# An S4 block and SwiGLU FFN on one core: eight blocks of two token tiles in place of two of two and four of three

## The chip, the cores and the metric

One core of one Trainium2 chip. The metric is the device time in microseconds, as the median of several runs. Engines: TensorE (PE, with PEld for its weight loads), VectorE (DVE), ScalarE (ACT), GpSimd (POOL), and SyncE (SP), which here only issues DMAs.

## What is computed

2048 tokens of 448 channels pass through a state-space convolution and then a gated feed-forward network (FFN), each behind a layer norm that is modulated by a condition c.

```python
sa, ca, ga, sb, cb, gb = (silu(c) @ w_mod) in six parts
h = layernorm(x) * (1 + ca) + sa
x = x + ga * (causal_conv(h, K(A, B, C, dt)) + h * Dskip)
h = layernorm(x) * (1 + cb) + sb
x = x + gb * ((silu(h @ w_gate) * (h @ w_up)) @ w_down)      # 448 -> 1792 -> 448
```

## The kernel before, in words

The tokens are 16 tiles of 128. `BLOCKS` (L26) groups them into blocks, `TILES` (L27) lists each block's tiles, and `MB` (L28) sizes the buffers for the largest block. The FFN goes through its 1792 hidden units in NF = 14 groups of 128, called f.

**The FFN of one block** is `ffn` (L736). For each f, `gate_up` (L741) makes gate and up: 22 products on TensorE (L758) with weights as the stationary operand and the block's transposed tokens as the moving one, 256 columns wide for two tiles and 384 for three. Tokens and weights are split into a high and a low part, so there are 7 products with `hhi` and 4 with `hlo` for each of the two sides. They land in two PSUM buffers taken in turn from four (`bank`, L71). After them ACT takes silu (L773), DVE multiplies gate by up (L788), ACT rounds to `phi` (L795) and DVE makes the rest `plo` (L796). `down` (L800, L808) then multiplies the hidden units of the group before, f - 1, by the down weights: three products of 448 columns for each tile, summed over all f in one PSUM buffer `dn` for each tile. At the block's end DVE multiplies by the gate row and adds to x (L869, L870) and SP stores the tile (L871). A two-tile operand lies from column 32 of `hhi` and `hlo` on, a three-tile one from column 0 (`first_col`, L147).

**The last block** has another end. The down products of the last two groups are kept out of the running sum; `last_sums` (L820) adds the rest to x early, and `finish` (L826, products L836, sums L847) makes the remaining ones, the last tile in two column ranges A and B so that its store starts earlier.

**The next block's preparation** is threaded between these groups. `run_blocks` (from L885) fills a table `todo`: under (f, 0) stands what is issued between `gate_up(f)` and `down(f - 1)`, under (f, 1) what follows `down(f - 1)`. In the tuple `TIMES` a slot h means f = h // 2 and late part h % 2. An entry for a block has the slots of the first norm's statistics, of its root, and one list for each tile of the next block: the stages s0 to s5 of the convolution's recurrence (`small_path`, L941 to L1011) and then the second norm's statistics. Stage s4 has three TensorE products for each tile (L982 to L984). Stage s5 sends the running state to the next tile by a DMA (L1005). Block 0 uses the first entry, block 1 the second, later ones the third (L896).

**Transposed tokens** come in two ways. If an entry has two more elements (`late`), the second norm is finished for all tiles together, `make_xn` (L207) writes normalized rows, and `transposes` (L222) turns them on TensorE by 128x128 transposes (L227) after the last `gate_up`. Without them, each tile goes by itself: statistics and root at slot h, `make_xn` at h + 1, and `turn` (L233) at h + 2: DVE transposes 32x32 squares (L236), SP writes the tile to DRAM (L237) and reads it back in four pieces (L239). Then `split_turned` (L242) stands at f = 13 in place of `transposes`. Both end in `parts` (L218): ACT writes `hhi` (L219) and DVE writes `hlo` (L220), for each of four groups of channels.

**Order of the queues.** Each engine executes its instructions in the order written, and SP its DMAs: the loads of x for the next block at (0, 1), then the turns, then the stores at the block's end. A start-up part, before 31.7 us in the trace, makes the convolution's constants and the first block's tokens.

Of the kernel before, what the change touches and what calls it, by code (L numbers as in the profile page):

```python
# [16 lines left out]
L, D, N, F = 2048, 448, 256, 1792  # L17
# [4 lines left out]
NF = F // 128  # L22
NP0 = 3
WU = (14, 0)
NS = 3
BLOCKS = [2, 2, 3, 3, 3, 3]  # L26
TILES = [list(range(sum(BLOCKS[:b]), sum(BLOCKS[:b + 1]))) for b in range(len(BLOCKS))]  # L27
MB = max(BLOCKS)  # L28

TIMES = (
# [3 lines left out]
)  # L36

EXTRA = (1,)
# [18 lines left out]
def tile_kernel(ctx, tc, x, a_re, a_im, b_re, b_im, c_re, c_im, log_dt,  # L57
# [9 lines left out]

    DN = [psd.tile([128, 512], F32, name=f"dn{q}") for q in range(MB)]
    CV = psd.tile([128, 512], F32, name="cv")

    def bank():  # L71
        t = psg.tile([128, 512], F32, name="bank")
        return t
# [20 lines left out]

    xbuf += stage_d[0:2 * MB - 4]
    spare = stages_.rearrange("p q a b c -> p (q a b c)")
    t_of = [spare[:, q * 512:(q + 1) * 512] for q in range(2, 2 + MB + 1)]
    turned = spare[:, 1024:1024 + MB * 512].rearrange("p (q a k r) -> p q a k r", q=MB, a=4, k=4)
    xn_of = [t_of[q] for q in (2, 3, 1)]
    p_of = [spare[:, q * 512:q * 512 + MB * 128] for q in range(2)]  # L100

# [45 lines left out]
    first_col = lambda n: 32 if n == 256 else 0  # L147
    hhi = const.tile([128, 4, MB * 128], F32R)
    hlo = const.tile([128, 4, MB * 128], F32R)
# [584 lines left out]
    def run_blocks(pools, stages, first=None):  # L734
        work, hid = pools.work, pools.hid
        def ffn(ts, fresh, last, todo):  # L736
# [73 lines left out]
            m = len(ts) - 1  # L810
# [13 lines left out]
                    ve.tensor_tensor(xs[i], dn[q][:, 0:D], xs[i], op=OP.add)  # L824

            def finish():  # L826
                o = [bank(), bank(), CV, DN[0]]
                A, B = slice(0, 256), slice(256, D)
                part = [(0, slice(0, D)), (1, slice(0, D)), (m, A), (m, B)]

                def sums(f, ks):
                    (hi, lo), (wh, wl) = pp[f], wp[f]
                    for k in ks:
                        q, c = part[k]
                        for z, (u, v) in enumerate(((hi, wh), (hi, wl), (lo, wh))):
                            pe.matmul(o[k][:, c], u[:, q * 128:(q + 1) * 128], v[:, c],  # L836
                                      start=f == NF - 2 and z == 0, stop=f == NF - 1 and z == 2)

                sums(NF - 2, (0, 1))
                sums(NF - 1, (0,))  # L840
                sums(NF - 2, (2,))
                sums(NF - 1, (1, 2))
                sums(NF - 2, (3,))
                sums(NF - 1, (3,))
                for k, (q, c) in enumerate(part):
                    i = ts[q]
                    ve.tensor_tensor(xs[i][:, c], o[k][:, c], xs[i][:, c], op=OP.add)  # L847
                    if k == 2:
                        sc.dma_start(out[i * 128:(i + 1) * 128, c], xs[i][:, c])

            for f in range(NF):
# [13 lines left out]
            if last:  # L865
                return finish()
# [250 lines left out]
```

## Time and profile before

| | |
|---|---|
| median of 3 runs | 471.46 us (470.68 to 472.36) |
| profiled execution: time | 470.78 us |
| profiled execution: span | 469.0 us |
| mean granted TensorE clock | 0.997 |
| instructions | 7027 |
| DMA over the span | 31.24 MB, mean 67 GB/s |

The span runs from the first to the last instruction of the profiled execution. Three views are used: the profile's page (busy time of each engine and groups of equal instructions with count, busy us, mean ns, and the idle time before them), the chain of waits (each piece with start, length and line, in order of time), and the timeline of one engine. "out<-in" names the tiles; `raw` is also the name under which the buffers of hidden units and of turned tokens appear, since they lie in that tile. Starts on TensorE in the chain are up to 0.2 us later than in the timeline, because the chain counts from the modelled end of the piece before.

### The profile page before, as it was taken

The page shows a single profiled execution, that of the slowest core. Times are in us where ns is not written, and L with a number is a line of the kernel's source. Part 1 is how long each engine was busy: PE and PEld are TensorE (multiplying, and loading weights), DVE is VectorE, ACT ScalarE, POOL GpSimd, SP SyncE. Part 2 cuts the span into 40 slices and gives each one's busy share as a digit, 9 for nine tenths or more (in the row PEclk, how much of TensorE's full clock was granted, in tenths as well). Part 3 has the DMA queues.
Part 4 walks back from the last instruction along what each step waited for, and adds up shares of the span by engine and source line. Part 5 has one row for each costly group of instructions (what it writes and reads, how often), then busy time and mean ns, then how long its engine had stood idle before and what let it go on. Part 6 is the DMA issues. An engine that isn't in the chain of part 4 may idle for free.

```text
span 469.0 us, 7027 instructions
## 1 busy us (share of the span) xinstructions
PE 459.0 (98%) x2735; PEld 438.0 (93%) x2735; DVE 282.1 (60%) x539; ACT 160.5 (34%) x363; POOL 63.4 (14%) x88
## 2 busy tenths in 40 slices
PE   6899999999999999999999999999999999999995
PEld 4579999999999999999999999999999999999995
DVE  4888999778866447573754766374566543222225
ACT  5888666522343122233212223311223222221111
POOL 1232001000000223200022410003141000000000
PEclk9999999999999999999999999999999999999998
DMA  8976652110003000111300011130001112000001
GB/s 309 405 251 189 211 178 91 58 42 2 2 0 100 0 1 0 46 46 46 117 2 0 2 45 46 45 119 1 1 16 31 46 45 80 22 1 1 1 0 64
DMA packets 18778, 31.24 MB, mean 67 GB/s; under 512 B 2608, under 2 KB 13488, under 8 KB 18736
## 3 DMA queue, kind: packets, MB, share of 16 engines
q1 hardware_dynamic: 18096, 30.53, 19.3%
q8 instruction: 23, 0.38, 0.4%
q10 hardware_dynamic: 640, 0.18, 0.2%
q14 instruction: 19, 0.16, 0.1%
HBM read 24.61 MB, written 6.03 MB: 65 GB/s over the span
## 4 chain that ended last, share of the span: by engine, by line
PE 95%; issue 2%; DMA 1%; POOL 0%; ACT 0%; DVE 0%; POOLq 0%; ACTq 0%
PE bank L758 61%; PE dn L808 28%; DMA vec<-in_c_log_dt_dram 1%; PE dn L480 1%; PE bank L983 1%; PE cv L982 1%; PE bank L836 1%; PE cv L984 1%; PE bank L227 0%; PE bank L266 0%; PE bank L403 0%; PE cv L995 0%; PE bank L437 0%; ACT L339 0%; PE cv L375 0%
## 5 line engine op out<-in xcount | busy, mean ns | idle before, releaser
L758 PE MATMUL bank<-hhi,gu 128*128 128x384 f32 (+1 forms) x1176 | 208.9, 317 | 0.1
L758 PEld LDWEIGHTS bank<-hhi,gu 128*128 128x128 f32 x1176 | 189.4, 188 | 3.0 <-issue 0.8
L758 PE MATMUL bank<-hlo,gu 128*128 128x384 f32 (+1 forms) x672 | 130.8, 317 | 0.0
L758 PEld LDWEIGHTS bank<-hlo,gu 128*128 128x128 f32 x672 | 109.1, 188 | 0.2
L788 DVE TENSOR_TENSOR bank<-raw,bank 128x384 f32<-128x384 f32 (+1 forms) x69 | 36.9, 534 | 117.9 <-PE bank L758 115.4
L795 ACT CAST phi<-bank 128x384 fp32r<-128x384 f32 (+1 forms) x83 | 36.7, 443 | 137.9 <-DVE bank L788 137.9
L773 ACT ACTIVATE raw<-bank 128x384 f32<-128x384 f32 (+1 forms) x70 | 32.8, 469 | 119.4 <-PE bank L758 103.7
L796 DVE TENSOR_TENSOR plo<-bank,phi 128x384 fp32r<-128x384 f32 (+1 forms) x83 | 42.5, 512 | 37.5 <-ACT phi L795 37.5
L808 PE MATMUL dn<-wdh,phi 128*128 128x448 f32 x218 | 57.6, 365 | 0.0
L808 PE MATMUL dn<-wdh,plo 128*128 128x448 f32 x218 | 57.2, 363 | 0.0
L808 PE MATMUL dn<-wdl,phi 128*128 128x448 f32 x218 | 56.9, 362 | 0.0
L808 PEld LDWEIGHTS dn<-wdh,plo 128*128 128x128 f32 x218 | 40.8, 187 | 3.0 <-DVE plo L796 0.3
L808 PEld LDWEIGHTS dn<-wdl,phi 128*128 128x128 f32 x218 | 40.9, 187 | 2.7
L808 PEld LDWEIGHTS dn<-wdh,phi 128*128 128x128 f32 x218 | 38.7, 188 | 1.6 <-ACT p L773 0.2
L185 POOL TENSOR_SCALAR rsb<-mvb 128x1 f32<-128x1 f32 (+2 forms) x13 | 4.4, 337 | 142.6 <-DVE mvb L157 142.6
L125 DVE TENSOR_TENSOR gu<-raw,gu 128x1024 fp32r<-128x1024 f32 x14 | 17.0, 1218 | 0.9 <-ACT gu L123 0.9
L185 POOL TENSOR_SCALAR rsa<-mva 128x3 f32<-128x3 f32 (+1 forms) x6 | 2.3, 380 | 98.4 <-DVE mva L157 96.1
L957 POOL TENSOR_TENSOR m<-m,gm 128x448 f32<-128x448 f32 x9 | 10.4, 1155 | 20.8 <-DVE m L202 17.1
L971 DVE TENSOR_TENSOR vl<-m,vh 128x448 fp32r<-128x448 f32 x12 | 9.1, 757 | 6.7 <-ACT vh L970 6.1
L122 ACT CAST gu<-raw 128x768 fp32r<-128x768 f32 x14 | 11.6, 832 | 0.0
L976 POOL TENSOR_TENSOR m<-m,gd 128x448 f32<-128x448 f32 x9 | 11.5, 1281 | 0.0
L215 ACT ACTIVATE raw<-raw,rsb 128x64 f32<-128x64 f32 x14 | 4.8, 345 | 18.9 <-DVE raw L212 9.7
(237 smaller groups left out, 411.7 us busy)
## 6 DMA issues: line engine op xcount, KB each, us to landing
raw<-in_B_w_gate_up_dram SPq DMA_DIRECT2D x14, 512.0 KB, 3.8
rawd<-in_B_w_down_dram SPq DMA_DIRECT2D x16, 224.0 KB, 3.9
x<-in_A_u_dram SPq DMA_DIRECT2D x12, 224.0 KB, 2.8
out_dram<-x SPq DMA_DIRECT2D x11, 224.0 KB, 1.9
xd<-raw SPq DMA_DIRECT2D x9, 256.0 KB, 2.0
raw<-xd SPq DMA_DIRECT2D x36, 64.0 KB, 1.9
wm<-in_w_mod_groups_dram SPq DMA_DIRECT2D x5, 448.0 KB, 8.2
wm<-in_w_mod_groups_dram SPq DMA_DIRECT2D x5, 336.0 KB, 8.2
```

The lines of the kernel that those rows point to most:

```text
L122: sc.copy(wgu[j][:, :, 0:3, :], w[:, :, 0:3, :])
L125: ve.tensor_tensor(wgu[j][:, :, 3:7, :], w[:, :, ::-1, :], f32(wgu[j][:, :, 0:4, :][:, :, ::-1, :]), op=OP.subtract)
L185: po.tensor_scalar(rs[:, 0:n], self.mv[:, 0:n, 1], EPS, None, op0=OP.add)
L758: pe.matmul(ps[s][:, 0:n], w[:, s, a], (hlo if lo else hhi)[:, k, first_col(n):first_col(n) + n], start=first and q == 0, stop=end and q = ...
L773: sc.activation(p[:, 0:n], ps[0][:, 0:n], AF.Silu)
L788: ve.tensor_tensor(ps[1][:, 0:n], p[:, 0:n], ps[1][:, 0:n], op=OP.mult)
L795: sc.copy(hi[:, 0:n], ps[1][:, 0:n])
L796: ve.tensor_tensor(lo[:, 0:n], ps[1][:, 0:n], f32(hi[:, 0:n]), op=OP.subtract)
L808: pe.matmul(dn[q][:, 0:D], u[:, cs], v, start=f == 0 and z == 0, stop=f == (NF - 3 if last else NF - 1) and z == 2)
L957: (ve if on_v else po).tensor_tensor(v, h, g, op=OP.mult)
L971: ve.tensor_tensor(vl, v0, f32(vh), op=OP.subtract)
L976: (ve if on_v else po).tensor_tensor(h, h, gd, op=OP.mult)
```

## The change

All blocks have two tiles, so there are eight blocks instead of six. `MB` stays 3, and so do all buffers. The first entry of `TIMES`, for block 0, is the same. The second, for block 1, loses its last two elements and its third tile, so block 2 is now prepared by `turn` and `split_turned` like the later ones; the third entry has the same slots as the second. `finish` is written for any number m + 1 of tiles: m whole tiles in banks, then the two column ranges of the last tile in CV and DN[0]. With two tiles its product order is: tile 0 of group 12, tile 0 of group 13, range A of groups 12 and 13, range B of groups 12 and 13.

```diff
-BLOCKS = [2, 2, 3, 3, 3, 3]
+BLOCKS = [2] * 8
 TILES = [list(range(sum(BLOCKS[:b]), sum(BLOCKS[:b + 1]))) for b in range(len(BLOCKS))]
-MB = max(BLOCKS)
+MB = 3
...
 TIMES = (
     ((1, 3), 5, ((5, 10, 13, 15, 15, 16), (9, 9, 17, 19, 20, 20)), 20, (22, 23)),
-    ((2, 3, 3), 3, ((5, 6, 8, 10, 10, 11, 13), (7, 8, 14, 15, 17, 17, 18), (13, 17, 17, 18, 20, 21, 21)), 23, (23, 23, 23)),
-    ((2, 3, 3), 3, ((5, 6, 8, 9, 10, 11, 12), (7, 8, 13, 14, 15, 16, 17), (11, 12, 18, 18, 20, 21, 21))),
+    ((2, 3), 3, ((4, 5, 7, 8, 10, 11, 12), (7, 8, 13, 14, 16, 17, 18))),
+    ((2, 3), 3, ((4, 5, 7, 8, 10, 11, 12), (7, 8, 13, 14, 16, 17, 18))),
 )
...
             def finish():
-                o = [bank(), bank(), CV, DN[0]]
+                o = [bank() for _ in range(m)] + [CV, DN[0]]
                 A, B = slice(0, 256), slice(256, D)
-                part = [(0, slice(0, D)), (1, slice(0, D)), (m, A), (m, B)]
+                part = [(q, slice(0, D)) for q in range(m)] + [(m, A), (m, B)]
...
-                sums(NF - 2, (0, 1))
+                sums(NF - 2, range(m))
                 sums(NF - 1, (0,))
-                sums(NF - 2, (2,))
-                sums(NF - 1, (1, 2))
-                sums(NF - 2, (3,))
-                sums(NF - 1, (3,))
+                sums(NF - 2, (m,))
+                sums(NF - 1, range(1, m + 1))
+                sums(NF - 2, (m + 1,))
+                sums(NF - 1, (m + 1,))
                 for k, (q, c) in enumerate(part):
                     i = ts[q]
                     ve.tensor_tensor(xs[i][:, c], o[k][:, c], xs[i][:, c], op=OP.add)
-                    if k == 2:
+                    if k == m:
                         sc.dma_start(out[i * 128:(i + 1) * 128, c], xs[i][:, c])
```

## The prediction

> **What bounds the kernel now.** I read the page's first table, then the chain that ended last, then the timeline of VectorE (DVE) and ScalarE (ACT) around a block's end.
>
> ```profile
> span 469.0 us, 7027 instructions
> PE 459.0 (98%) x2735; PEld 438.0 (93%) x2735; DVE 282.1 (60%) x539; ACT 160.5 (34%) x363; POOL 63.4 (14%) x88
> PE 95%; issue 2%; DMA 1%; POOL 0%; ACT 0%; DVE 0%; POOLq 0%; ACTq 0%
> ```
>
> TensorE (PE) is busy for 98% of the span and carries 95% of the chain. So two questions decide: how long TensorE's own instruction list becomes, and whether somewhere in the shorter blocks another engine comes late enough to stop it. The chain in order of time answers the first (start us, length us, what, products); x22 is one pass of gate and up over one group f of 128 hidden units, L808 the products of `down`, L227 the transposes.
>
> ```profile
> 88.49 5.18 PE bank L758 x44
> ...
> 94.88 2.52 PE bank L758 x22
> ...
> 106.02 2.52 PE bank L758 x22
> 109.14 1.20 PE dn L808 x6
> ...
> 140.07 0.33 PE bank L227 x3
> ...
> 141.60 2.41 PE dn L808 x12
> 144.01 7.63 PE bank L758 x44
> 151.64 1.80 PE dn L808 x9
> ...
> 385.47 7.63 PE bank L758 x44
> ```
>
> Block 1 (two tiles) runs from 88.49 to 144.01, 55.52 us. Blocks 2 to 4 (three tiles) run from 144.01 to 385.47, 241.46 us or 80.49 us each. The last block's products start at 385.47.
>
> **The change part by part.** All differences below are of TensorE's time unless said otherwise.
>
> *Passes of gate and up.* A three-tile pass takes 7.63 / 2 = 3.815 us. From 94.88 to 106.02 lie three full steps of f (one pass and one `down` each), 11.14 / 3 = 3.713 us; less the `down` of 1.20 a two-tile pass is 2.513 us. The four three-tile blocks hold 4 x 14 = 56 passes, 213.6 us; the six two-tile blocks that replace them hold 84, 211.1 us. So more, shorter passes are slightly cheaper here: three passes of 2.513 are 7.54, two of 3.815 are 7.63. Term: **-2.5 us**. Each pass adds its silu, product, cast and difference on ACT and DVE, hidden beside TensorE as long as they are in time (below).
>
> Beside the row of 2.513 the Trainium skill, "TensorE: Matmul & The Clock Gate", section "Back-to-back issue gap", speaks against this term: an isolated product of N columns costs about N/2.4 + 2.5 ns warm, a fixed part for each product. By that (an estimate from that page) 22 products cost 2.40 us at 256 columns and 3.57 us at 384, the exchange +1.6 in place of -2.5, and the whole change about +1.0. The rows disagree with its sign: 114.2 ns for 256 columns and 173.4 for 384.
>
> *Products of `down`.* 1.80 us for nine and 1.20 for six are both 0.20 each; their number doesn't change. Nothing.
>
> *State products* (s4, three for each tile). Between 108.54, the end of the pass at 106.02, and 109.14 they take 0.60 us. Twelve tiles before and after. Nothing.
>
> *Transposes.* Block 2 was prepared in block 1 by 12 transposes on TensorE, from 140.07 to 141.60: **-1.53 us**. In their place block 1 now does what the later blocks do. Its costs elsewhere:
>
> ```profile
> L236 DVE STREAM_TRANSPOSE raw<-raw 128x512 f32<-128x512 f32 x9 | 6.4, 706 | 3.5 <-ACT raw L216 3.5
> xd<-raw SPq DMA_DIRECT2D x9, 256.0 KB, 2.0
> raw<-xd SPq DMA_DIRECT2D x36, 64.0 KB, 1.9
> 143.85:224.33 80.48, 80.48 (x444) 78.73 (x443) 45.10 (x82) 21.53 (x44) 14.74 (x17) 1.00 0.11 35
> ```
>
> The number of turned tiles goes from 9 to 12: three more of 0.71 us on DVE, and 3 writes and 12 reads more on SP's queue. In that queue the turn stands behind the block's two loads of x and ahead of its two stores; nothing else waits there. The second tile is turned at f = 10 and used at f = 13: three steps, 11.1 us, for 2.0 + 1.9 us of landing and four issues. Hidden; with that cover gone a whole landing of 1.9 us would show at each block's end. DVE's 45.10 us for three tiles and 80.48 us are 56% (third number of the row); two tiles in about 53 us keep about that share. Hidden on average; the order within a step is the question.
>
> *The block's end.* This happens six times with the turned path in place of three. After the last pass ACT and DVE must write hhi and hlo of the next block while TensorE has only two `down`s as cover: 12 x 0.20 = 2.4 us, against 3.6 before. At 256 columns the end of block 0 shows what they need:
>
> ```profile
> 85.87 0.42 DVE L788 TENSOR_TENSOR bank<-p,bank 128x256 f32<-128x256 f32 x1
> ...
> 86.32 0.37 ACT L795 CAST phi<-bank 128x256 fp32r<-128x256 f32 x1 [0.75 <-DVE bank L788]
> 86.59 0.48 ACT L219 ACTIVATE hhi<-bank,sbc 128x256 fp32r<-128x256 f32 x1
> 87.31 0.85 ACT L219 ACTIVATE hhi<-bank,sbc 128x256 fp32r<-128x256 f32 x2
> ...
> 87.90 0.87 DVE L220 SCALAR_TENSOR_TENSOR hlo<-bank,sbc,hhi 128x256 fp32r<-128x256 f32 x2
> ```
>
> Counted from L788's start (85.87), the last hhi is there at 2.29 and the last hlo at 2.90. L788 starts about 0.26 after TensorE has gone on to the next products (460.64 against 460.38 in the finish, below), so the new pass begins at 2.40 - 0.26 = 2.14. Its k = 3 part of hhi comes six products of 0.114 later, at 2.83, and the last hlo ten products later, at 3.28. Margins 0.54 and 0.38 us: no stop. Term 0; bounds 0 and, if the sources in SBUF or a semaphore cost the margin and as much again, 0.4 each, 2.4 in all.
>
> *A slower pace at a block's start.* The two passes at 88.49 took 5.18 us, not 2 x 2.513 = 5.03. No wait stands beside them, so I don't know what sets this pace. Six more two-tile blocks start with such a pair: between 0 and 6 x 0.15 = 0.9. I take **+0.5**, the middle: the pair shown is the nearest row, but it follows transposes, which the others don't.
>
> *The queues at f = 6 and 7.* make_xn of the first tile and s2 of the second stand in one step there. Three-tile block 2 shows the chain:
>
> ```profile
> 182.69 0.18 DVE L157 BATCH_NORM_AGGREGATE mvb<-stb 128x2 f32<-128x6 f32 x1
> ...
> 183.76 0.80 POOL L186 TENSOR_TENSOR rsb<-rsb,halves 128x1 f32<-128x1 f32 x1
> 184.59 0.35 ACT L215 ACTIVATE raw<-raw,rsb 128x64 f32<-128x64 f32 x1 [3.06 <-POOL rsb L186]
> 185.55 0.55 ACT L970 CAST vh<-m 128x448 fp32r<-128x448 f32 x1
> 186.13 1.16 DVE L971 TENSOR_TENSOR vl<-m,vh 128x448 fp32r<-128x448 f32 x1 [1.48 <-ACT vh L970]
> 187.22 0.55 DVE L788 TENSOR_TENSOR bank<-raw,bank 128x384 f32<-128x384 f32 x1
> ```
>
> and the groups give the usual sizes of two of its operations (busy us, mean ns):
>
> ```profile
> L971 DVE TENSOR_TENSOR vl<-m,vh 128x448 fp32r<-128x448 f32 x12 | 9.1, 757 | 6.7 <-ACT vh L970 6.1
> L156 DVE BATCH_NORM_STATS2 stb<-x 128x6 f32<-128x448 f32 x10 | 6.3, 626 | 0.3
> ```
>
> DVE sits behind ACT, ACT behind POOL's root, and L788 of the next group is queued behind all of it, 187.22 - 182.87 = 4.35 us after the statistics. In a two-tile step those end about 2.1 after L788 of f = 6 (0.42 for it, about 0.42 for the cast, 0.42 for the difference, then 0.63 and 0.18), so L788 of f = 7 starts at about 6.4 and phi is there 0.42 + 0.37 later, at 7.2. TensorE wants it at 2 x 3.71 - 0.27 = 7.15. That is on the edge. The row's 1.16 for vl overlapped POOL's s1 of a third tile, which is gone; with the mean of 0.76, phi comes at 6.8, margin 0.3. Term 0, bounds 0 and 0.2 in six blocks, 1.2.
>
> *The finish.* The closing sums hold 2 tiles instead of 3: six products move from the closing sums into ordinary `down`s, no change in sum. But only three of them, 0.60 us, now stand between the last pass and the first that needs the last phi, where there were six.
>
> ```profile
> 460.38 0.37 PE L836 MATMUL bank<-wdh,phi 128*128 128x448 f32 x1
> ```
>
> ```profile
> 460.64 0.49 DVE L781 TENSOR_TENSOR raw<-raw,bank 128x128 f32<-128x128 f32 x2 [0.38 <-PE bank L758]
> 460.96 0.50 ACT L782 CAST phi<-raw 128x128 fp32r<-128x128 f32 x2 [1.75 <-DVE raw L781]
> ```
>
> The cover would end at 460.38 + 0.60 = 460.98, and the first phi ends about 0.28 after 460.96 (two of them take 0.50, overlapping): **+0.4** with the weight load behind it (bounds 0.2 and 0.6).
>
> Sum: -2.5 - 1.53 + 0.5 + 0.4 = **-3.1 us**. The profiled execution's time of 470.78 becomes 467.7 (span 469.0 to 465.9). The median of the runs shown, 471.46, lies 0.68 above that execution and becomes **468.4**.
>
> **The rivals.**
>
> *Slow pace throughout (slower).* All two-tile passes run as the pair at 88.49, 2.59 us: 84 x 2.59 = 217.6, +4.0 in place of -2.5, with -1.5 and +0.4 a total of +2.9: **474.4**. This decides from the point where more than 3.1 / 0.08, about 40 more of the 84 passes, are slow. For it: the only back-to-back pair in the trace is slow, and no row names the cause. Against it: by 94.88 block 1 is back at 2.52, and the pace is held to 106.02 and beyond. Chance 0.10, including a mix of slow passes and stops that ends above.
>
> *The covers fail (no change).* The block's end costs 0.4 six times or the f = 6 chain 0.2 to 0.5 each time: +2.4 at about the middle, total -0.7: **470.8**. For it: margins of 0.4 us are thin beside operations of 0.4 to 1.2 us, and every wait is in order. Against it: block 1 already runs three tiles' state work in two-tile steps, and the chain there gives no wait of TensorE. Chance 0.14.
>
> *The full exchange (faster than forecast).* No slow pairs, a finish of +0.2: -3.8, **467.7**. It belongs to the forecast's range.
>
> *A fixed price for each product (no change).* The 616 products more could each cost as much beyond their columns as the long ones do: at the 3.815 / 8448 = 0.4516 ns of a column in a three-tile pass, a two-tile pass would take 2.543, and any price above that turns the term round; with 0.02 us more for each of 84 passes the total is +1.1: **472.5**. Against it: 2.513 was measured in two-tile steps. Chance 0.03, inside the 0.14 of no change. The Trainium skill's rule above ends there as well.
>
> *The edit doesn't do what it says.* Not here: the list of tiles sets the loop, and the passes must go from 6 x 14 = 84 to 8 x 14 = 112.
>
> **How the numbers follow.** About 0.3%, 1.4 us, is what a measurement of this kernel can tell from no change. Forecast 0.76 (faster by 1.4 to 4.5), no change 0.14, slower 0.10. The range: lower end -4.0 of the two sure terms and 0.8 for the spread of runs, 466.6; upper end the forecast with the rest of the slow pairs (0.4), the finish (0.2), half of the block's ends (1.2) and of the f = 6 chain (0.6), -0.7 in all, 470.8, which I put at 470.9 and which takes in about half of the no-change case.
>
> **What would show it.** Right: passes of 2.51 in the chain after 94.88, blocks 53.2 to 53.4 us apart (55.52 - 1.53 - 0.60 = 53.39 for block 1), only the eight transposes before block 1 at L227, twelve at L236, TensorE still at 98%, closing sums from about 458.0 (460.38 - 3.53 + 1.2, since six products move ahead of them), and span near 465.9. Wrong on pace: passes of 2.59 far into a block. Wrong on the block's end: TensorE waiting for L219 or L220 ahead of an x44. Wrong on f = 6: TensorE's weight load of L808 waiting for L795 near the middle of each block. Wrong on the finish: no gap, or more than 0.6, ahead of the fourth closing product.

## The result and the profile after

The changed kernel takes **467.97 us** (median of 4 runs, 466.79 to 468.45) against 471.39 (4 runs, 470.68 to 472.36): ratio 0.9919, 95% interval 0.9896 to 0.9943, so 3.4 us faster. The profiled execution took 466.79 us with a span of 465.0; 468.4 was predicted.

The page of the changed kernel, busy time by engine:

```profile
span 465.0 us, 8481 instructions
PE 455.5 (98%) x3339; PEld 433.7 (93%) x3339; DVE 293.5 (63%) x600; ACT 170.6 (37%) x426; POOL 74.4 (16%) x99
```

There are 604 more products, but TensorE is busy 3.5 us less: its list has more and shorter entries, and it still sets the time. The chain that ended last shows each block's start and the closing end of one block (start, length, what, products):

```profile
88.37 5.18 PE bank L758 x44
...
139.31 2.47 PE dn L808 x12
141.78 5.18 PE bank L758 x44
...
195.18 5.00 PE bank L758 x44
...
248.38 5.18 PE bank L758 x44
...
408.38 5.00 PE bank L758 x44
```

The transposes ahead of block 2 are gone: 139.31 goes straight over to 141.78. Blocks are 53.20 or 53.40 us apart, inside the forecast 53.2 to 53.4, and which of the two depends on the pair of passes at the start, 5.00 or 5.18. Summed from each group's first product to the next group's in the two traces, from block 1's first product to the last closing product:

| TensorE, us | before | after | difference | forecast |
|---|---|---|---|---|
| passes of gate and up (block 1 on) | 248.99 | 246.50 | -2.49 | -2.5 + 0.5 |
| transposes ahead of block 2 | 1.46 | 0 | -1.46 | -1.53 |
| `down` and closing sums | 117.96 | 118.67 | +0.71 | +0.4 |
| state products | 7.29 | 7.23 | -0.06 | 0 |
| together | 375.70 | 372.40 | -3.30 | -3.1 |

Two pieces lie outside this stretch: block 1's first product comes at 88.21 instead of 88.33, and from the last closing product to the span's end there are 4.40 us instead of 4.98. Together these make 469.0 into 465.0. In the profiled executions that share block 0 (before, after, e1, e2, e5, e6 and e11) block 1 began anywhere between 88.2 and 89.2, so the medians' 3.4 us is a better figure for the change than the 4.0 of two single profiles. A part of the 3.4 lies outside the span: in e11, the changed kernel run again, the median span fell by 2.9 us (469.2 to 466.3) and the median time by 3.3.

What TensorE's weight loads waited for in the changed kernel, from 80 us on (us in all, times, longest); the last row lies at the end of block 0:

```profile
PEld dn L808 <- ACT phi L795: 0.9, 6, 0.2
PEld bank L836 <- ACT phi L782: 0.6, 1, 0.6
PEld dn L808 <- DVE plo L796: 0.3, 1, 0.3
```

Nothing waits for hhi or hlo, and nothing near f = 6. The six short waits for phi lie at the ends of blocks 1 to 6. This is the first of them, on ACT, DVE and TensorE's weight loads:

```profile
139.40 0.43 DVE L788 TENSOR_TENSOR bank<-raw,bank 128x256 f32<-128x256 f32 x1 [2.41 <-PE bank L758]
139.87 0.37 ACT L795 CAST phi<-bank 128x256 fp32r<-128x256 f32 x1 [1.32 <-DVE bank L788]
140.14 1.71 ACT L219 ACTIVATE hhi<-raw,sbc 128x256 fp32r<-128x256 f32 x4
140.68 1.68 DVE L220 SCALAR_TENSOR_TENSOR hlo<-raw,sbc,hhi 128x256 fp32r<-128x256 f32 x4
...
140.29 0.30 PEld L808 LDWEIGHTS dn<-wdh,phi 128*128 128x128 f32 x2 [0.16 <-ACT phi L795]
```

The last hhi is there at 141.85 and the last hlo at 142.36, 2.45 and 2.96 after L788 (forecast 2.29 and 2.90); by the forecast's sum TensorE wants them at 2.83 and 3.28. These margins held. What TensorE waits for is the last group's own phi. It ends at 140.24, and only one `down` of 1.2 us stands between the last pass and the `down` that needs it, so that weight load stands for 0.16 us.

### The profile page after: what moved, and what is told of

It reads as the page before. It is cut to its first block, busy times and chain, and to the rows that moved or that the text cites. A ratio compares the mean times of both kernels' runs of the same rounds, so it can differ in the third digit from the quotient of the medians.

```text
span 465.0 us, 8481 instructions
## 1 busy us (share of the span) xinstructions
PE 455.5 (98%) x3339; PEld 433.7 (93%) x3339; DVE 293.5 (63%) x600; ACT 170.6 (37%) x426; POOL 74.4 (16%) x99
## 4 chain that ended last, share of the span: by engine, by line
PE 94%; issue 2%; DVE 1%; DMA 1%; ACT 1%; POOL 0%; DVEq 0%; POOLq 0%; ACTq 0%
PE bank L758 60%; PE dn L808 28%; DMA vec<-in_c_log_dt_dram 1%; PE dn L480 1%; PE cv L982 1%; PE bank L983 1%; PE cv L984 1%; PE bank L266 0%; PE bank L403 0%; PE cv L995 0%; PE bank L437 0%; ACT L339 0%; DVE x L824 0%; PE cv L375 0%; DVE dn L823 0%
## 5 line engine op out<-in xcount | busy, mean ns | idle before, releaser
L758 PE MATMUL bank<-hhi,gu 128*128 128x256 f32 x1568 | 216.7, 278 | 0.1
L758 PEld LDWEIGHTS bank<-hhi,gu 128*128 128x128 f32 x1568 | 204.0, 188 | 3.7 <-issue 0.8
L758 PE MATMUL bank<-hlo,gu 128*128 128x256 f32 x896 | 138.8, 277 | 0.0
L758 PEld LDWEIGHTS bank<-hlo,gu 128*128 128x128 f32 x896 | 118.6, 188 | 0.2
L788 DVE TENSOR_TENSOR bank<-raw,bank 128x256 f32<-128x256 f32 x97 | 41.4, 426 | 98.3 <-PE bank L758 85.5
L795 ACT CAST phi<-bank 128x256 fp32r<-128x256 f32 x111 | 41.4, 373 | 139.8 <-DVE bank L788 139.8
L796 DVE TENSOR_TENSOR plo<-bank,phi 128x256 fp32r<-128x256 f32 x111 | 47.0, 424 | 44.0 <-ACT phi L795 44.0
L773 ACT ACTIVATE raw<-bank 128x256 f32<-128x256 f32 x98 | 37.6, 384 | 93.0 <-PE bank L758 89.2
L185 POOL TENSOR_SCALAR rsb<-mvb 128x1 f32<-128x1 f32 (+1 forms) x15 | 8.8, 585 | 115.4 <-DVE mvb L157 115.4
L957 POOL TENSOR_TENSOR m<-m,gm 128x448 f32<-128x448 f32 x10 | 11.6, 1155 | 25.6 <-DVE m L202 25.6
L963 DVE TENSOR_TENSOR v<-v,run 1x448 fp32r<-1x448 f32 x14 | 13.3, 951 | 0.0
```

The costliest lines, as they stand in the source:

```text
L185: po.tensor_scalar(rs[:, 0:n], self.mv[:, 0:n, 1], EPS, None, op0=OP.add)
L758: pe.matmul(ps[s][:, 0:n], w[:, s, a], (hlo if lo else hhi)[:, k, first_col(n):first_col(n) + n], start=first and q == 0, stop=end and q = ...
L773: sc.activation(p[:, 0:n], ps[0][:, 0:n], AF.Silu)
L788: ve.tensor_tensor(ps[1][:, 0:n], p[:, 0:n], ps[1][:, 0:n], op=OP.mult)
L795: sc.copy(hi[:, 0:n], ps[1][:, 0:n])
L796: ve.tensor_tensor(lo[:, 0:n], ps[1][:, 0:n], f32(hi[:, 0:n]), op=OP.subtract)
```

## The experiments

Each was timed beside the kernel before, on the same chip as that. They ran on three chips in all, so their ratios to the kernel before are given. The changed kernel, run again with them (e11), gave 468.08 us.

**Which part gives the gain.** e1 keeps the old blocks and turns block 2, with the slots of the later blocks; e2 keeps the new blocks and only gives block 2 its transposes back.

```diff
 e1, on the kernel before: the second entry of TIMES becomes a copy of the third
-    ((2, 3, 3), 3, ((5, 6, 8, 10, 10, 11, 13), (7, 8, 14, 15, 17, 17, 18), (13, 17, 17, 18, 20, 21, 21)), 23, (23, 23, 23)),
+    ((2, 3, 3), 3, ((5, 6, 8, 9, 10, 11, 12), (7, 8, 13, 14, 15, 16, 17), (11, 12, 18, 18, 20, 21, 21))),
 e2, on the changed kernel: the second entry
-    ((2, 3), 3, ((4, 5, 7, 8, 10, 11, 12), (7, 8, 13, 14, 16, 17, 18))),
+    ((2, 3), 3, ((4, 5, 7, 8, 10, 11, 12), (7, 8, 13, 14, 16, 17, 18)), 20, (21, 22)),
```

> The old blocks of two and three tiles, with one thing of the change: block 2 is turned by VectorE and through DRAM instead of by 12 transposes. My sum: the 12 transposes (1.46 us from the first of them to the next product) leave TensorE's list and nothing else changes, so about 1.5 us under the kernel before, span about 467.5. Rival, that the turned path carries the whole gain (a shorter block end as well as no transposes): 3 us or more under it. Rival, that three tiles' turns in two-tile steps come too late: TensorE waits ahead of block 2 and the gain is under 1 us.

> The changed kernel, but block 2 is again prepared by transposes on TensorE (8 of them). My sum: 0.8 to 0.9 us of transposes come back, and the short wait for phi at that one block end goes, so the span is 0.7 to 0.9 us over the changed kernel's. If the passes' width carries the gain, the kernel stays about 2.5 to 3 us under the kernel before; if the turned path carries it, it comes back to within 1 us of it.

e1 took 477.91 us against 470.96, ratio 1.0134 (1.0112 to 1.0156): slower, by the third case and by far more than it said. First TensorE's first long wait, in the middle of block 1 (timeline), then the chain at block 1's end, where the last of three turned tiles comes late:

```profile
120.55 0.47 PE L982 MATMUL cv<-vh,tri 128*128 128x448 f32 x1 [2.15 <-ACT vh L970]
```

```profile
147.10 2.08 DMA raw<-xd
...
150.18 9.90 PE bank L758 x44
```

The chain into the first wait runs over DVE and then ACT:

```profile
117.25 0.51 DVE m L957
117.77 0.54 DVE v L957
118.30 0.61 DVE raw L212
...
119.37 0.67 ACT raw L216
120.04 0.46 ACT vh L970
```

In block 1 the kernel gives s1 and s3 to DVE, in later blocks to POOL (L1010), and e1 puts the later blocks' slots on it. So s1 of the third tile (L957) and `make_xn` of the first (L212, L216) stand ahead of `vh` of the second, TensorE's state products start 2.15 us late, and block 2 waits for a turn that lands at 149.18. After each wait TensorE also runs slower for a while (stretches of the span, us; busy us and count of TensorE, its weight loads, DVE, ACT and POOL; then the granted clock and the DMA's share and GB/s):

```profile
114.50:117.00 2.50, 2.50 (x23) 2.49 (x23) 2.03 (x5) 0.37 (x1) 0.00 (x0) 1.00 0.00 0
121.75:125.40 3.65, 3.65 (x23) 3.65 (x22) 2.17 (x4) 0.53 (x2) 0.00 (x0) 0.65 0.19 72
...
150.20:157.80 7.60, 7.60 (x32) 6.97 (x33) 5.38 (x10) 2.42 (x5) 0.00 (x0) 0.78 0.35 110
```

The granted clock, third from the end, is 1.00 before, 0.65 over the 3.65 us behind the first wait, 0.78 over the 7.60 us behind the second. In the same trace it is 0.50 from 120.9 to 124.3 and from 151.6 to 155.0. An estimate from these rows: waits of 2.15 and 2.0 us and half of twice 3.4 us sum to 7.6 us; less the 1.5 of the transposes that is 6.1 of the 7.0 us lost. So with these slots the dropped transposes aren't worth 1.5 us under the old blocks: three tiles' stages and turns don't fit into block 1's two-tile steps. The kernel before does fit three tiles' stages there, without the turns and with slots of its own; other slots for three turned tiles weren't tried.

e2 took 469.47 us, ratio 0.9962 (0.9945 to 0.9978): slower than the changed kernel (e11) by 1.4 us, where the sum said 0.7 to 0.9, and by the ratio still 1.8 us (1.0 to 2.6) under the kernel before, where 2.5 to 3 were expected. The transposes stand there again:

```profile
139.79 0.22 PE bank L227 x2
...
140.66 2.41 PE dn L808 x12
```

From 139.79 to 140.66 that is 0.87 us. The profile shows no further wait. The forecast was one of the span, and there it nearly holds: the median span of e2 is 466.95 us, against 466.15 in e5 on the same chip, which is the changed kernel but for two buffers left unused, and 466.3 in e11 on another. The rest lies outside the span: the time is 2.4 to 2.9 us longer than the span in e2's runs and 1.8 to 1.9 in those of e5 and e11; why, no run shows. Both parts count, and the passes are the larger.

**Why a two-tile pass is cheap.** The forecast took 2.51 from the trace without a reason. Column 32 of `first_col` is the one thing in which two-tile operands differ beside their width.

```diff
 e3, on the changed kernel; e8_col16 and e8_col64 have 16 and 64 in place of 32
-    first_col = lambda n: 32 if n == 256 else 0
+    first_col = lambda n: 0
 e4, on the kernel before: tokens and all that lies behind them 32 columns further on
-    first_col = lambda n: 32 if n == 256 else 0
-    hhi = const.tile([128, 4, MB * 128], F32R)
-    hlo = const.tile([128, 4, MB * 128], F32R)
+    first_col = lambda n: 0
+    both = const.tile([128, 8 * MB * 128 + 32], F32R)
+    hhi, hlo = (both[:, 32 + z * 4 * MB * 128:32 + (z + 1) * 4 * MB * 128].rearrange("p (k c) -> p k c", k=4) for z in range(2))
 e9 on the kernel before, e10 on the changed one: only what lies behind the tokens
-    first_col = lambda n: 32 if n == 256 else 0
+    first_col = lambda n: 0
     hlo = const.tile([128, 4, MB * 128], F32R)
+    gap = const.tile([128, 32], F32, name="gap")
 e4, e9, e10, for room
-                p = hid.tile([128, 280], F32, name="p") if fresh else p_of[f % 2]
+                p = hid.tile([128, 256], F32, name="p") if fresh else p_of[f % 2]
```

(Block 0's own writers of hhi and hlo, L447 to L458, move with the column.)

> The changed kernel with the two-tile operand at column 0 of hhi and hlo instead of column 32. If the start column sets what a pass costs beyond its columns (about 17 of TensorE's cycles at 256 columns against 32 at 384), passes go from 2.51 us to about 2.59 or more, and 112 of them add 8 us or more, so that the exchange of three-tile for two-tile passes would lose. If the width alone sets it, passes stay at 2.51 and the span within 0.5 us.

> The changed kernel with the two-tile operand from column 16 in place of 32. If the start has to lie a certain distance from a row's beginning, passes come out at 2.59 as from column 0 (span 473 to 474); if any start other than 0 serves, at 2.51 (465 to 466).

> The changed kernel with the two-tile operand from column 64 in place of 32. If any start other than 0 serves, passes stay at 2.51 (span 465 to 466); if the place counts modulo 64 columns, they go to 2.59 (473 to 474). A pass under 2.50 would show a still better place.

> The kernel before with hhi and hlo moved on by 32 columns in SBUF, so that the three-tile operands (and the two-tile ones, from the same place) start 32 columns further on; nothing else of the work differs. If the start is what a cheap pass needs, three-tile passes fall from 3.815 us toward 3.69 (the 0.087 us that column 0 against 32 makes at two tiles, times 1.5), 56 of them save up to 7 us, and the kernel before would end under the changed one: then the width has nothing to do with the gain. If the width is what counts, they stay at 3.81 and the time within 1 us of before.

> The kernel before with all token operands from column 0 and everything behind hhi and hlo in SBUF, the weights above all, moved on by 32 columns (and the block-0 buffer p cut from 280 to 256 columns to make room). Theory: a pass's price hangs on the distance between weights and tokens in SBUF, taken modulo 64 columns, because moving both by 32 left three-tile passes at 3.815 and moving the weights alone made two-tile ones slow. Then two-tile passes stay at 2.51 here. For three tiles two outcomes: if they too have a cheap place, 3.815 falls toward 3.69, 56 passes save up to 7 us, and the kernel before beats the changed one: the gain was the place, not the number of tiles. If 384 columns have no cheap place, they stay at 3.81: the gain belongs to the two-tile width at its place. The moved phi buffers cost the down products about 1.2 us, as they did when tokens and weights moved together.

> The changed kernel with the same move of the weights and the tokens from column 0. If the distance between the two decides, passes are back at 2.51 although the tokens start at column 0, where they took 2.59 with the weights in their old place; the down products cost about 1.2 us more, so the span is 466 to 467. If the column itself decides, they take 2.59 and the span is 473 to 475.

e3 took 475.19 us, ratio 1.0080 (1.0058 to 1.0102): the change without column 32 is by this ratio 3.8 us *slower* than the kernel before. One run each of column 16 and 64 gave 478.39 and 475.70. The chains of e3, of column 16 and of column 64, in this order:

```profile
204.53 2.59 PE bank L758 x22
```

```profile
205.88 2.61 PE bank L758 x22
```

```profile
204.53 2.59 PE bank L758 x22
```

From block 1 on every pass takes 2.59 instead of 2.51, and 2.60 to 2.64 from column 16. That is the forecast's slow pace throughout, priced there at 474.4. That e3 came within 0.8 us of this is in part chance: the rival counted 84 slow passes, and in e3 those of block 1 and most of block 0 are slow too.

e4 took 473.64 us, ratio 1.0055 (1.0035 to 1.0075), and was a surprise: three-tile passes stayed as they were, and two-tile ones, whose tokens lie where they did, went slow. What had changed for them is that the weights lie 32 columns further on. (In e4, e9 and e10 `p` was cut as well, which moves the phi buffers against the down weights; e4's `down` products take 1.2 us more in sum.)

```profile
103.28 2.59 PE bank L758 x22
...
235.96 3.81 PE bank L758 x22
```

e10 and e9 therefore move the weights alone, with all tokens at column 0. The chain of e10, then of e9:

```profile
202.62 2.51 PE bank L759 x22
205.12 1.23 PE dn L809 x6
```

```profile
235.70 3.89 PE bank L759 x22
239.58 1.82 PE dn L809 x9
241.41 3.84 PE bank L759 x22
```

So it is the distance between weights and tokens in SBUF, and not the column by itself: tokens from column 32 with the weights in place, or from column 0 with the weights 32 columns on, both give 2.51. These two distances differ by 64 columns, so what counts is the distance modulo 64 columns, as far as these runs go. The distances that lie 32 columns off (e3, column 64, e4) give 2.59, and 16 columns off about 2.61. Three tiles gain nothing from the same move: 3.81 becomes 3.84 to 3.89. Only these two distances were tried for them, so whether 384 columns have a cheaper one is open.

e10 took 470.79 us in all (ratio 0.9988, 0.9974 to 1.0002; span 468.6 where 466 to 467 was expected): its `down` products, with the phi buffers moved against their weights, sum to 117.7 us instead of 115.8, and the passes to 247.9 instead of 246.5, because from block 1 on all pairs and the 12 single passes next after state products took the slow price. e9 took 476.40 (1.0096, 1.0075 to 1.0117). Why the distance matters inside TensorE no run shows.

**The slow pairs at a block's start.**

```diff
 e5, on the changed kernel
             down(NF - 1, qz)
+            bank(), bank()
             for q, i in enumerate(ts):
```

> The changed kernel with two PSUM buffers more taken (and not used) at each block's end, so that every block begins at the same one of the four in the rotation; a block takes 30 now, so they begin alternately two apart, and in the changed kernel's trace blocks 2, 4 and 6 begin with a slow pair of passes (5.18 us) and blocks 3, 5 and 7 with a fast one (5.00). If the place in the rotation decides, all six pairs come out alike: all fast, 0.55 us less, or all slow, 0.55 us more. If the phase is carried by time or by the instruction stream, the alternation stays.

> The changed kernel once more. Its first profile began blocks 2, 4 and 6 with a slow pair of passes; the one with only the closing sums in another order began all with a fast one. If the slow pairs come and go with the execution, the pattern differs here, between none and six (0 to 1.1 us). If they belong to the code, blocks 2, 4 and 6 are slow again. The time is 466.7 to 468.5 as before.

e5 took 467.94 us (0.9929, 0.9911 to 0.9947), e11 468.08 (0.9926, 0.9910 to 0.9941). In e5 all seven pairs were slow. In e11, the unchanged code once more, blocks 3, 5 and 7 were slow, where blocks 2, 4 and 6 had been in the first profile:

```profile
142.72 5.00 PE bank L758 x44
...
195.92 5.18 PE bank L758 x44
```

In e6 (below), with the rotation of the changed kernel, all pairs were fast. So neither the code nor the place in the buffers' rotation fixes it alone; it goes with the execution. A slow pair is two passes of 2.59, so at the good distance too a pass has two prices. At a bad one it can have the good price: in e3 two passes of block 0, each next after products of L995, took 2.50. What sets it is open, but its size is bounded: 0.18 us for each pair, at most 1.1 for six.

**The finish.**

```diff
 e6, on the changed kernel
-                sums(NF - 2, range(m))
-                sums(NF - 1, (0,))
-                sums(NF - 2, (m,))
-                sums(NF - 1, range(1, m + 1))
-                sums(NF - 2, (m + 1,))
-                sums(NF - 1, (m + 1,))
+                sums(NF - 2, range(m + 2))
+                sums(NF - 1, range(m + 2))
```

> The changed kernel with all three parts of group 12's closing sums ahead of all of group 13's: 1.27 us of products in place of 0.60 stand between the last pass and the first product that needs the last phi. The wait of 0.55 us in TensorE's weight loads there should go; the last product comes 0.4 to 0.55 us earlier, the first tile's store 0.2 us later, the span 0.4 us shorter. If the stores and not the products set the end, the span stays.

It took 467.72 us (0.9926, 0.9910 to 0.9942), not to be told from the changed kernel. The wait went, as the chain shows: products follow each other from 457.75 on.

```profile
457.75 0.60 PE bank L836 x3
...
459.00 0.64 PE bank L836 x3
```

The 18 closing products start within 2.43 us in place of 2.91. But the stores took it back. The first tile's store in the changed kernel, then in e6 (KB, us to landing):

```profile
out_dram<-x SPq DMA_DIRECT2D x1, 224.0 KB, 2.3
```

```profile
out_dram<-x SPq DMA_DIRECT2D x1, 224.0 KB, 3.2
```

All three stores now start within 0.6 us of each other, and each takes 3.2 us to land instead of 2.2 to 2.4. The second case of the expectation held. No version beat the changed kernel by more than the measurement shows.

## Why the prediction was right, step by step

- **Passes, -2.5.** Right as a price, and a little small: without the slow pairs it was -3.0. The 0.4 between is 0.005 us for each of 84 passes, less than the 0.01 to which the rows of the chain are read. But the reason behind it, "more, shorter passes are slightly cheaper", isn't one of width. At another distance between weights and tokens the same exchange costs 4 us (e3: 84 x 2.59 less 213.6). The trace of before couldn't tell this, since all its two-tile passes lay at the good distance. That the new blocks lie there too follows from `first_col`, but the forecast didn't ask for it; here it had luck. The *slow pace* rival had the other price right, 2.59, though not its cause.
- **The rule of the Trainium skill.** The fixed part for each product in "TensorE: Matmul & The Clock Gate", section "Back-to-back issue gap", would have made the exchange +1.6 us. It came out at -2.5, slow pairs included, and in e3, where it came out as a loss, the passes' price moved with the place of an operand and at an unchanged width. The runs decide against using it for this term.
- **Transposes, -1.53.** Measured 1.46, right for the changed kernel. That they go for nothing depends on the block having two tiles (e1).
- **Block's end, 0.** The margins of hhi and hlo held as worked out. The step left out the last group's own phi, for which TensorE's weight load now waits about 0.16 at each end, where three tiles had nine products for cover and the trace of before has no such wait; the rows of `down` grow by about 0.24 us in all.
- **Slow pairs, +0.5.** 3 x 0.18 = 0.54 in the profiled execution, and between 0 and 1.1 by execution, so that the term was met this closely is luck. The pair at 88.49 wasn't the only slow place in the trace of before; block 0 has three single passes at the same price:

```profile
62.77 2.60 PE bank L758 x22
...
66.58 2.59 PE bank L758 x22
...
82.62 2.59 PE bank L758 x22
```

- **DVE's share.** The forecast kept it at about 56%. It rose to 65% in block 1 (34.81 of 53.37 us) and 61% in block 2 (32.67 of 53.30), still without a wait of TensorE for DVE from block 1 on.
- **f = 6 and 7, 0.** The chain runs as drawn, but the margin was larger than the 0.3 forecast. Block 2 of the changed kernel:

```profile
169.99 0.35 ACT L215 ACTIVATE raw<-raw,rsb 128x64 f32<-128x64 f32 x1 [2.90 <-POOL rsb L186]
...
171.53 0.63 DVE L971 TENSOR_TENSOR vl<-m,vh 128x448 fp32r<-128x448 f32 x1 [1.46 <-ACT vh L970]
172.07 0.42 DVE L788 TENSOR_TENSOR bank<-raw,bank 128x256 f32<-128x256 f32 x1
172.53 0.37 ACT L795 CAST phi<-bank 128x256 fp32r<-128x256 f32 x1 [0.75 <-DVE bank L788]
...
173.81 0.38 PEld L808 LDWEIGHTS dn<-wdh,phi 128*128 128x128 f32 x2
```

  phi is there at 172.90 and its weight load comes at 173.81: 0.91 to spare. The step forgot that the second tile's state products, 0.6 us, stand ahead of that `down`; and vl took 0.63, where the forecast had the mean of 0.76.
- **Finish, +0.4.** Measured 2.91 - (3.64 - 6 x 0.20) = +0.47. TensorE's weight load waited 0.55 us for the first phi.
- **Not in the sum.** The end behind the last product was 0.58 us shorter in the profile, with two tiles' stores in flight instead of three (2.4 us to land against 3.0). Other executions with this two-tile end had 4.3 to 4.8 us there, and those with a three-tile end 4.9 to 5.5. That the number of stores is the cause is only argued.

## What to carry to other kernels

When TensorE is busy all through, price a new blocking by passes of that width in the same trace, then ask what else those passes have in common: here the distance of the operands in SBUF decided the sign. A shorter block needs its covers counted again, down to the last group's own result, and slots that work in one block can fail in another (e1). At the end of a kernel a wait that goes from TensorE may come back in the stores.

## What the runs showed of the hardware

- The distance in SBUF between the weights and the moving operand changes what a product of 256 columns costs, in nearly all passes: 22 products in 2.51 us at the good distance, 2.59 when it is off by 32 columns of float32, about 2.61 when off by 16. Two distances that differ by 64 columns both gave 2.51.
- A single wait of 2.15 us in TensorE was followed by a mean granted clock of 0.65 over a stretch of 3.65 us, 0.50 from 120.9 to 124.3 us (e1). The Trainium skill, "TensorE: Matmul & The Clock Gate", section "Why this matters for your kernels", gives gaps of more than about 3 us as the ones to avoid; here a shorter one was enough.
